# Copying z between partitions in two transfers of eight partitions instead of one of sixteen

## Chip, cores and metric

The kernel runs on one core of one Trainium2 chip. The metric is the device time of one execution in microseconds (us), less is better; three timed runs of the kernel before took 440.68, 440.70 and 441.16 us, median 440.7. Engines are named as in the profile: PE is TensorE's matmul side and PEld its weight loads, DVE is VectorE, ACT is ScalarE, POOL is GpSimd, SP is SyncE. SP computes nothing here; it only issues transfers. "16 engines" in what follows are the core's DMA engines, which carry the transfers of every queue.

## What is computed

Two stages, cut to what matters here:

```python
# stage 1: linear attention, 8 batches x 8 heads x 576 rows x 64
q_p, k_p = phi(q), phi(k)                    # exp of a projection and of its negative
kv = einsum('bhsf,bhsd->bhfd', k_p, v);  z = k_p.sum(axis=2)
x = (q_p @ kv) / (q_p @ z)                   # -> (8, 576, 512)
# stage 2: mix 64 frequencies, then add a ReLU of a channel product
X = rfft(x, axis=1)[:, :64]                  # 64 modes
Y[m] = X[m] @ (w_r[m] + 1j * w_i[m])         # one 512x512 complex matrix per mode
u = x + irfft(Y, n=576, axis=1)
out = u + relu(u @ w_ch)
```

The 64 matrices pairs `w_r`, `w_i` are 134 MB of the 164 MB that the core reads, so they stream from memory during nearly the whole kernel.

## The kernel before

**Stage 1** (lines 503 to 573) runs over 16 units (4 groups of two heads times 4 pairs of batches), and mixes of the first two channel groups are interleaved with it.

**Stage 2** (lines 779 to 1022) works on eight blocks of eight modes, `o` = 0 to 7. The weights come in tiles `wt` of 1 MB (128 partitions, bf16, cast on the way from fp32), loaded by `wload` (line 340) on POOL's queue; `next_w` (line 359) issues the next one each time that a `mix` (line 461) has used one and its buffer is free. A `mix` is eight matmuls and needs one `wt`. When the last of a block's mixes is done (`g == 3`, `i == 1`, line 943), the block's result is finished: DVE adds the partial sums into `yst` (128 partitions x 512, bf16; a partition is one of 16 mode components times one of eight batches), PE transposes it, multiplies it with `w_ch` and ACT and DVE put the product into `zst` (lines 971 to 979), of the same shape. So `yst` is Y of this block and `zst` is Y times `w_ch`.

**The copies between partitions.** The inverse transform sums over modes, so the modes of all blocks must lie along partitions and the batches beside them. `put` (line 816) does this with a transfer on SP's queue: the 128 partitions of `zst` (1 KB each) become 16 partitions of `zall`, `16 * o` to `16 * o + 15`, with the eight batches in a row (16 x 8 x 512). Each destination partition takes the rows of eight source partitions. `put` is called for `yst` into `yall` (line 952) and for `zst` into `zall` (line 980). Blocks 0 to 6 are copied so (seven copies of y, seven of z); blocks 6 and 7 also go into `yl`, block 6 on POOL's queue and block 7 on SP's.

**The readers.** `Absorb.sum_q` and `only_w` (lines 737 and 764) multiply `zall` by the tables `CI` or `CD` of the inverse transform: with 96 partitions (blocks 0 to 5) for most output rows, with 112 (block 6 too) for the first rows. The results are added to `xw`, which holds x times `w_ch`. They are in the list `todo` (line 807), which `fill` works off in portions between the mixes. PE executes in program order, so the first matmul that reads `zall` stops PE until every copy of blocks 0 to 5 has landed. The kernel ends with the output rows, added and stored by `Last` (lines 825 to 914) after the last mix.

**Order.** Every engine keeps program order (`InOrder`, line 27); a helper records all operations, so the profile names line 37 for nearly all of them and it is read by tiles. SP's queue issues, after the first loads, the copies of y and z in turn, the four of `yl`, and then the stores of the output.

The lines that the change is about:

Of the kernel before, what the change touches and what calls it, by code (L numbers as in the profile page):

```python
# [43 lines left out]
def kernel(  # L44
# [15 lines left out]
    pool, sp = InOrder(tc, nc.gpsimd), InOrder(tc, nc.sync)  # L60
# [530 lines left out]
    zall = pw.tile([128, B_, DMODEL], BF16, name="zall", tag="wt")  # L591
# [222 lines left out]
                todo.pop(0)()  # L814

    def put(src, o, dst, copies):
        if o < 7:
            sp.dma_start(dst[16 * o:16 * o + 16], src)
        if o > 5:
            for s in copies:  # L820
                r = 32 * s + 16 * (o - 6)
                (pool if o == 6 else sp).dma_start(yl[r:r + 16], src)
# [100 lines left out]
    while mixq:  # L923
        key = mixq.pop(0)
        g, o, i = key[0], key[1] // 2, key[1] % 2
# [17 lines left out]
        if g == NG - 1 and i == 1:  # L943
# [5 lines left out]
            for h in range(2):  # L949
                dve.tensor_tensor(out=yst[:, H * h:H * h + H], in0=py[:, H * h:H * h + H],  # L950
                                  in1=yacc[:, o, H * h:H * h + H], op=ALU.add)
            put(yst, o, yall, (0, 2))
            if o < 5:
                fill(min(n, 1))
# [23 lines left out]
            act.copy(zst[:, cut[0]], pz[0])  # L978
            dve.tensor_copy(zst[:, cut[1]], pz[1])
            put(zst, o, zall, (1, 3))  # L980
            fill(max(n - 2, 0) if o < 5 else n)
        else:
# [71 lines left out]
```

## Time and profile before

| | before |
|---|---|
| three timed runs, median (lowest to highest) | 440.7 us (440.68 to 441.16) |
| span of the profiled execution | 440.0 us |
| what the timed runs have over that span | 0.7 us |
| PE busy | 326.7 us, 74% |
| DVE, ACT, POOL busy | 296.0, 279.1, 112.5 us |
| HBM read, written | 163.64 MB, 9.44 MB |
| z copies into `zall` on SP | 7, 128 KB each, issued from 326.31 to 387.02 us |
| one z copy: issue on SP, issue to landing | 547 ns, 6.4 us (median) |
| first matmul that reads `zall` | 373.86 us |
| last load of a `wt`: issue, landing | 369.69 us, 404.6 us |

The span is that of one execution that the hardware profiler recorded; it gives no other time for that execution, and the timed runs are other executions. All times inside the kernel are microseconds from the start of the span. The page lists busy time by engine, the transfers by queue, and the chain of work that ended last; the timeline lists instructions in order, with the idle time before each and what ended it. The trace also keeps a record of each packet that the DMA engines moved (its queue, start, duration and bytes, but not which engine moved it) and, for each transfer, of 16 landing events.

### The profile page before, as it was taken

What the parts mean: (1) busy time and instruction counts of PE and PEld (TensorE: products, weight loads), DVE (VectorE), ACT (ScalarE), POOL (GpSimd) and SP (SyncE); (2) the same over time, 40 slices, a digit from 0 to 9 for tenths busy, and PEclk for the clock granted to TensorE, in tenths of its full rate; (3) what the DMA queues carried; (4) which work ended last, traced back from release to release, by engine and by line L of the source; (5) the groups of instructions that cost most, each with busy time, mean ns of one, the idle gap of its engine ahead of it and who ended that gap; (6) DMA issues with size and microseconds to landing.
All of it is one profiled execution on the core that took longest, in us unless ns stands there. A gap on an engine that the chain in (4) does not pass through costs nothing.

```text
span 440.0 us, 10106 instructions
## 1 busy us (share of the span) xinstructions
PE 326.7 (74%) x4190; PEld 199.7 (45%) x4233; DVE 296.0 (67%) x583; ACT 279.1 (63%) x478; POOL 112.5 (26%) x151
## 2 busy tenths in 40 slices
PE   1676668787678687778787777174679998997993
PEld 0445546555455455455455455051435454333320
DVE  5568787567785777886886878243883334885684
ACT  2788887687896777885875876210644442764782
POOL 6232132132211222221222121121101121582072
PEclk9989988689998799896896999675999999999997
DMA  8999999999999999999999999999999999996787
GB/s 193 210 211 210 237 212 238 231 217 241 235 211 239 221 230 234 237 213 235 228 221 238 210 235 209 236 209 212 212 215 223 220 221 223 206 218 150 238 361 310
DMA packets 51710, 99.55 MB, mean 226 GB/s; under 512 B 2512, under 2 KB 13648, under 8 KB 51664
## 3 DMA queue, kind: packets, MB, share of 16 engines
q0 software_dynamic: 45232, 85.86, 99.6%
q1 hardware_dynamic: 6432, 13.04, 8.5%
q8 instruction: 33, 0.54, 0.4%
q14 instruction: 13, 0.11, 0.1%
HBM read 163.64 MB, written 9.44 MB: 393 GB/s over the span
## 4 chain that ended last, share of the span: by engine, by line
PE 32%; DMA 31%; DVE 15%; ACT 15%; issue 5%; POOL 0%; POOLq 0%; ACTq 0%; DVEq 0%
DMA wt<-in_moe_w_i_dram 14%; PE pt L37 13%; PE one L37 12%; DMA wt<-in_moe_w_r_dram 8%; DMA vn<-in_v_dram 7%; ACT AB L37 6%; PE two L37 6%; DVE m L37 4%; DVE mk L37 4%; ACT AQ L37 3%; DMA qb<-in_q_dram 2%; PE pp L37 2%; ACT XT L37 2%; ACT qT L37 2%; DVE xw L37 1%
## 5 line engine op out<-in xcount | busy, mean ns | idle before, releaser
L37 ACT ACTIVATE AB<-two 128x1024 bf16<-128x1024 f32 x64 | 62.1, 1026 | 12.5 <-DVE mk L37 10.1
L37 ACT ACTIVATE AQ<-two 128x1024 bf16<-128x1024 f32 x64 | 62.7, 1046 | 1.3 <-PE two L37 1.2
L37 ACT CAST xw<-pt 128x512 bf16<-128x512 f32 x50 | 29.3, 587 | 42.3 <-PE pt L37 42.2
L37 DVE TENSOR_TENSOR va<-vn,ee 128x1152 bf16<-128x1152 f32 x32 | 42.0, 1355 | 11.9 <-DMA vn<-in_v_dram 11.9
L37 DVE TENSOR_REDUCE m<-two 128x8 f32<-128x1024 f32 x32 | 39.1, 1223 | 14.9 <-PE two L37 14.6
L37 DVE TENSOR_REDUCE mk<-two 128x8 f32<-128x1024 f32 x32 | 38.9, 1218 | 9.8 <-PE two L37 9.8
L37 POOL DMA_DIRECT2D wt<-in_moe_w_i_dram x28 | 20.9, 748 | 88.0 <-PE pt L37 36.2
L37 POOL DMA_DIRECT2D wt<-in_moe_w_r_dram x30 | 22.5, 749 | 72.3 <-PE one L37 29.3
L37 PE MATMUL pt<-wchb,xT 128*128 128x512 bf16 x127 | 34.7, 385 | 5.7 <-DVE xT L37 4.2
L37 PEld LDWEIGHTS <-xs 128*128 128x128 bf16 x624 | 31.3, 102 | 12.5 <-issue 7.5
L37 PE MATMUL two<-w2blk,qT 128*128 128x256 bf16 x128 | 21.9, 298 | 19.7 <-ACT AB L37 8.8
L37 ACT COPY qT<-one 128x512 bf16<-128x512 bf16 (+1 forms) x32 | 19.2, 641 | 26.4 <-PE one L37 26.2
L37 PE MATMUL one<-wt,XT 128*32 128x512 bf16 x304 | 27.7, 456 | 5.7 <-DMA wt<-in_moe_w_i_dram 4.1
L37 PE MATMUL one<-va,AB 64*128 64x65 bf16 x1024 | 23.1, 200 | 10.9 <-DVE va L37 10.9
L37 PEld LDWEIGHTS <-qT 128*128 128x128 bf16 x144 | 14.4, 102 | 36.7 <-issue 33.3
L37 PE MATMUL two<-mT,minus 96*128 96x512 bf16 x64 | 27.0, 423 | 3.4 <-issue 1.3
L37 DVE COPY xT<-pt 128x512 bf16<-128x512 bf16 x36 | 17.0, 472 | 17.3 <-PE pt L37 17.3
L37 PEld LDWEIGHTS <-AQ 128*128 128x128 bf16 x512 | 24.5, 108 | 8.2 <-issue 4.7
L37 PEld LDWEIGHTS <-XT 128*32 128x32 bf16 x512 | 14.7, 149 | 29.5 <-issue 23.2
L37 PE MATMUL one<-kvz,AQ 128*128 128x65 bf16 x512 | 27.2, 208 | 1.1 <-ACT qT L37 0.8
L37 DVE TENSOR_TENSOR xs<-one,rd 128x384 bf16<-128x384 f32 x48 | 26.8, 557 | 1.6
L37 PEld LDWEIGHTS <-AB 64*128 64x128 bf16 x1024 | 20.7, 101 | 15.0 <-DVE va L37 9.3
(151 smaller groups left out, 700.5 us busy)
## 6 DMA issues: line engine op xcount, KB each, us to landing
wt<-in_moe_w_r_dram POOLq DMA_DIRECT2D x30, 1024.0 KB, 28.6
wt<-in_moe_w_i_dram POOLq DMA_DIRECT2D x28, 1024.0 KB, 29.1
out_dram<-of SPq DMA_DIRECT2D x16, 512.0 KB, 3.7
vn<-in_v_dram POOLq DMA_DIRECT2D x14, 576.0 KB, 25.0
kb<-in_k_dram POOLq DMA_DIRECT2D x16, 288.0 KB, 22.0
qb<-in_q_dram POOLq DMA_DIRECT2D x16, 288.0 KB, 20.5
xs<-in_moe_w_i_dram POOLq DMA_DIRECT2D x2, 1024.0 KB, 24.1
vn<-in_v_dram SPq DMA_DIRECT2D x2, 576.0 KB, 6.7
```

The source lines that it names most:

```text
L37: ins = f(*args, **kwargs)
```

## The change

```diff
     def put(src, o, dst, copies):
-        if o < 7:
+        if o < 7 and dst is zall:
+            for h in range(2):
+                sp.dma_start(dst[16 * o + 8 * h:16 * o + 8 * h + 8], src[64 * h:64 * h + 64])
+        elif o < 7:
             sp.dma_start(dst[16 * o:16 * o + 16], src)
```

Each of the seven copies of z is issued as two transfers on SP's queue, one behind the other: the first takes source partitions 0 to 63 into the first eight destination partitions of the block, the second takes 64 to 127 into the other eight. The bytes and their places are the same, and the copies of y are as before.

In the order of instructions on the engines this adds seven transfers to SP's list, each directly behind its first half, and changes nothing else in the order of PE, DVE, ACT and POOL. The waits change in name and in number: what read `zall` or reused `zst` waited for one transfer and now waits for two.

## The prediction, made before the changed kernel was run

> **What bounds the kernel now.** I read the page first. Its third part gives the transfers by queue (packets, MB, share of 16 engines' time):
>
> ```profile
> q0 software_dynamic: 45232, 85.86, 99.6%
> q1 hardware_dynamic: 6432, 13.04, 8.5%
> q8 instruction: 33, 0.54, 0.4%
> ```
>
> q0 is POOL's queue, the inputs and weights. It is busy in 99.6% of the span, so the kernel is a stream of loads with a tail behind it. q1 is SP's queue, which carries the copies of y and z. Next the chain of work that ended last, in order of time (start, duration, what):
>
> ```profile
> 369.41 0.28 issue
> 369.69 34.91 DMA wt<-in_moe_w_i_dram
> 404.61 0.04 issue
> 404.65 0.69 PE pt L37 x8
> ```
>
> The last weight tile is issued at 369.69 and lands at 404.6, and the last mix starts at once. From there to the end are 440.0 - 404.6 = 35.4 us, in which no weight is loaded. The tile itself takes some 5 us; 35 is the queue ahead of it. So it is not its issue that counts but how fast the 16 engines work off q0. **What slows the slowest engine by 1 us puts the end 1 us later.**
>
> The landing events of that tile show how unequal the engines are: 398.0, 398.5, 398.8, 399.5, 400.0, 400.1, 400.1, 401.8 us, and then 403.2, 403.3, 403.6, 403.8, 403.8, 404.0, 404.1, 404.6. Eight engines lead, eight lag by some 4 us. The stretches of time show the same (us, busy of PE, PEld, DVE, ACT, POOL, then PEclk, DMA share, GB/s):
>
> ```profile
> 398.00:399.00 1.00, 1.00 (x6) 0.42 (x5) 0.98 (x3) 0.77 (x3) 0.78 (x1) 1.00 1.10 240
> 401.00:402.00 1.00, 1.00 (x7) 0.40 (x5) 0.60 (x2) 0.58 (x1) 0.00 (x0) 1.00 0.62 125
> 402.00:403.00 1.00, 0.36 (x2) 0.08 (x1) 0.44 (x1) 0.52 (x1) 0.00 (x0) 1.00 0.62 129
> 405.00:406.00 1.00, 0.47 (x10) 0.11 (x2) 0.64 (x2) 0.00 (x0) 0.00 (x0) 1.00 0.09 25
> ```
>
> The share is 1.10 with all engines at work and 0.62 from 401 on: nearly half of them have nothing left. The cause is in the packet records: q8's 33 packets, 16 KB and some 0.95 us each, recur in durations with a period of eight (936, 975, 975, 961, 893, 893, 948, 945 ns), so the same eight engines carry them; after each, one landing of the running tile moves back by about 1.1 us (after the first, at 33.85, one goes from 0.8 to 1.9 us behind the earliest). Four rounds make the 4 us.
>
> **What a z copy costs an engine.** The packet records around the copy at 326.31 and the others: a copy is 128 packets of 1024 bytes and 16 of 4 bytes. With 16 landing events per copy that is 8 + 1 for each engine, the packets of one destination partition. While it runs, packets of q0 and q1 alternate on an engine: q0's 2048-byte packets follow each other every 154 ns, with a z packet between them every 208. So a z packet takes 54 ns from the weights, a copy 8 x 54 + 9 = 0.44 us from each engine.
>
> **The change part by part.**
>
> *Issue.* Seven more instructions on SP, 0.55 us each. Two transfers in a row take 1.19 us (the yl copies), so the second half starts some 0.6 us after the first. Closest behind it is the copy of y at 327.85, after z at 326.31: 326.31 + 1.19 = 327.5, no delay. SP waits for other engines all through this stretch, so this costs nothing. SP also waits for the eighth transfer before its own on each semaphore; with three transfers a block instead of two that one is over two blocks (some 18 us) old, and landed. The reuse of `zst` waits for both halves, but two blocks later: nothing. With issues 2 us apart any of these would cost a part of 0.6 us.
>
> *Which engines carry a half.* No transfer in the trace has eight destination partitions, so I bound it. All of them have 16, 64 or 128, and 16 equal shares. One end: each half is again cut into 16 shares, 4 + 1 packets an engine; over both halves only the seven extra 4-byte packets are new, 7 x 9 = 63 ns. Other end: an engine takes whole destination partitions, as in the copy before. Then a half fills eight engines with 8 + 1 packets and leaves eight out, and, if the second half takes the same eight, these pay 2 x 0.44 us a copy and the others nothing. I take the second end, as the nearest row is the z copy itself, one partition to an engine. All seven copies come before the last tile has landed, so those eight engines lose 7 x 0.44 = **3.1 us**, and the other eight gain 3.1. If the halves took different eights, nothing would change but the latency.
>
> The Trainium skill states a rule for this (DMA: Bandwidth & Descriptors, "Why a DMA increments its semaphore by 16 and not by 1"): the number of engines is the largest one up to 16 that divides the outermost dimension of both sides, and on SP's queue they are the lowest-numbered. By it both halves use the same eight, which is the 3.1 us end; no row here shows it. The same page's rules for kernel authors speak the other way: two transfers to disjoint halves of the partitions are no use since both spray over all 16 engines; by that the sum is the 63 ns.
>
> *Do these eight lag or lead?* The records don't name engines. If any of them is in the lagging half, the last tile lands later by up to 3.1 us (1.7 if only the earliest of the laggards is hit: 403.2 + 3.1 - 404.6). If they are the leading eight, their last landing is 401.8 + 3.1 = 404.9 and the laggards' 404.6 - 3.1 = 401.5: 0.3 later in all. One weak row: where I could follow an engine from its landing event to its first z packet, laggards started 134 ns after the burst's first packet (mean of 11), leaders 163 (of 12). If engines are served in order, laggards stand somewhat earlier, and a transfer that fills only eight would fill the first. I take the laggards.
>
> *Latency of a copy.* It matters at one place, block 5 (start, duration, what):
>
> ```profile
> 365.06 0.55 SPq L37 DMA_DIRECT2D yall<-yst  x1
> 367.06 0.55 SPq L37 DMA_DIRECT2D zall<-zst  x1
> ```
> ```profile
> 373.52 0.41 PE L37 MATMUL pt<-yall,CI 96*64 96x512 bf16 x2 [0.57 <-DVE xs L37]
> 373.86 0.39 PE L37 MATMUL pp<-zall,CI 96*128 96x512 bf16 x1
> 403.12 0.59 PE L37 MATMUL pp<-xs,CF 128*128 128x512 bf16 x2 [0.75 <-ACT xw L37]
> 404.65 0.66 PE L37 MATMUL pt<-wt,XT 128*32 128x512 bf16 x8 [0.94 <-DMA wt<-in_moe_w_i_dram]
> ```
>
> A copy lands 6.3 to 6.6 us after its issue; its packets take the last 1.7 (8 x 208 ns). z of block 5 is there at 373.5, the first reader starts at 373.86. On the same eight engines the second half's packets follow the first's: 1.7 us later, 375.3. So PE, in program order, gets a **new wait of 1.4 us** there, with the sums of all rows and the next mixes behind it, and ACT, DVE and POOL behind those. Until the last mix PE has 0.94 + 0.22 us of waiting for weights to give back (the latter at 399.64). 0.3 us would be left. But where the last tile comes 3.1 us later, PE has those too, and the wait costs nothing. Also without the wait, PE can't gain much by weights that come early: at most the 0.94.
>
> *Sum.* Last tile 404.6 + 3.1 = 407.7. PE would be ready: copies of block 5 issued up to 1.2 us later because their weights come late, first reader 2.8 later, less 1.2 returned, still 1.5 us ahead of the tile. Behind the tile nothing changes: 35.4 us. Span 440.0 + 3.1 = 443.1; the timed runs lie 0.7 above it, 440.7 + 3.1 = **443.8 us**.
>
> **The rivals.** About 0.2% (0.9 us) is what a measurement of this kernel can tell from no change.
>
> *Laggards hit (forecast), 65%:* 442.4 to 444.8, likeliest 443.8. For it: 16 equal engines without slack in q0, and half of them or less idle at the end.
>
> *Not slower: the leading eight carry z, 20%.* Mechanism: they have 3 to 4 us to give at the last tile, and the laggards are relieved. What is left is 0.3 us of the PE wait or of the last leader: 441.0. It decides as long as the load stays under the gap of 3 to 4 us. For it: nothing in the trace says which engines lag.
>
> *The split does not concentrate, 11%:* 16 shares, or different eights. Each engine moves the same bytes; 63 ns; the two halves land about as one copy did: 440.7, at most 441.0.
>
> *Faster, 4%:* leaders carry z, no wait at 373.86, the tile early: PE's 0.94 us are returned, 439.8.
>
> **How the numbers follow.** Slower 0.65 is the first case, same 0.31 the second and third, faster 0.04. The forecast is the likeliest case; its own range is 442.4 to 444.8. The range of 8 in 10 must take in the cases near no change, from 440.5.
>
> **What would show it.** Right: each half of z with eight landings or 64 packets on half of the engines; the last `wt` landing near 407.7, its 16 landings 6 to 9 us apart where they were 6.6; a wait before the first reader of `zall`, or before mixes from 374 on, and a longer one before the last mix; a tail of 35.4 us as before. Wrong: a z half spread over 16 engines; the landings of the last tile drawn together (leaders loaded); a last tile at 404.6 with a later end, which would put the loss on PE. Everything up to 326 us must be as before.

## The result, and the profile after

The changed kernel takes 445.63 us (median of four runs, 444.89 to 447.41) where the kernel before takes 440.93 (four runs, 440.68 to 442.33). The ratio is 1.0107, with a 95% interval of 1.0084 to 1.013: 4.7 us slower. Forecast were 443.8 us, with a range of 440.5 to 444.8; the direction holds and the size does not.

The profiled execution of the changed kernel has a span of 444.1 us, 4.1 more than that of before, and a time of its own of 445.85 us. Every run for which both are listed has 1.75 us between span and time, not the 0.7 that the prediction took from two different executions. By this the profiled execution of the kernel before would have taken some 441.7 us (an estimate), 0.8 more than its median, which is why the traces differ by less than the medians.

The page's third part for the changed kernel (packets, MB, share of 16 engines):

```profile
q0 software_dynamic: 45232, 85.86, 99.0%
q1 hardware_dynamic: 6432, 13.04, 8.8%
```

Packets and bytes are the same, and the load stream is as dense as before within 0.6 points. The chain that ended last, though, no longer runs over a weight tile. The same stretch of it (start, duration, what):

```profile
366.44 7.75 DMA zall<-zst
374.19 2.06 issue
376.25 0.58 PE pp L37
...
392.28 9.23 DMA zall<-zst
401.51 0.04 issue
...
408.98 0.62 PE pt L37 x8
```

Where the last `wt` load stood (34.91 us), there are now two z copies, of block 5 and of block 6, and between them PE, DVE and ACT. So PE's order sets the end, not the weights. SP's line for the z copy of block 5, and then PE's lines around the first readers of `zall` and the mixes (in brackets the idle time before, and what ended it):

```profile
366.44 1.27 SPq L37 DMA_DIRECT2D zall<-zst  x2
```
```profile
372.92 0.41 PE L37 MATMUL pt<-yall,CI 96*64 96x512 bf16 x2 [0.56 <-DVE xs L37]
376.25 0.58 PE L37 MATMUL pp<-zall,CI 96*128 96x512 bf16 x1 [2.92 <-issue]
...
401.55 0.38 PE L37 MATMUL pt<-zall,CI 112*128 112x512 bf16 x1 [0.79 <-DMA zall<-zst]
...
408.91 0.66 PE L37 MATMUL pt<-wt,XT 128*32 128x512 bf16 x8
```

The first reader of `zall` had no wait before; it now has 2.92 us. The line puts it down to "issue", so it does not name what ended the wait; the landing events do: PE's last matmul was over at 373.3, the first half had landed by 374.2, and the second half's eight landings come from 375.55 to 376.05, just ahead of the reader. The matmul itself takes 0.58 us where it took 0.39, and the mix behind it, at 376.76, takes 1.08 where it took 0.66. The reader of block 6's copy waits 0.79 us. The last mix starts at 408.91 without a wait for its tile, where it had waited 0.94.

Why these matmuls are slower is in the granted clock. In the trace its record changes only in steps of 3.413 us. Cut along these steps, the stretches of the changed kernel are (us, busy of PE, PEld, DVE, ACT, POOL, then PEclk, DMA share, GB/s):

```profile
371.78:375.20 3.42, 0.98 (x5) 0.29 (x3) 1.89 (x3) 0.00 (x0) 0.00 (x0) 1.00 1.23 196
375.20:378.61 3.41, 2.36 (x12) 0.55 (x12) 0.00 (x0) 0.78 (x2) 0.00 (x0) 0.50 1.13 214
378.61:382.02 3.41, 3.41 (x10) 1.19 (x9) 1.29 (x2) 2.11 (x4) 0.67 (x1) 0.50 1.13 213
382.02:385.43 3.41, 3.41 (x23) 1.07 (x21) 2.88 (x5) 2.22 (x4) 2.39 (x3) 1.00 1.12 211
```
The kernel before, one step at the same place:
```profile
373.56:376.98 3.42, 3.34 (x21) 1.28 (x21) 1.87 (x4) 1.70 (x4) 0.00 (x0) 1.00 1.13 213
```

After the step in which PE stood idle, its clock is 0.50 for two steps, 6.8 us: 10 matmuls fit into a full step in place of 21 to 23. The kernel before has no half clock between 309 and 435 us. This is a second loss behind the wait, and the prediction had no term for it.

Two of the stretches that the prediction showed for the load stream, in the changed kernel:

```profile
402.00:403.00 1.00, 1.00 (x6) 0.47 (x5) 0.60 (x1) 0.55 (x1) 0.26 (x1) 1.00 0.70 133
...
405.00:406.00 1.00, 1.00 (x11) 0.39 (x12) 0.75 (x2) 0.75 (x3) 0.00 (x0) 1.00 0.28 82
```

The DMA share is 0.28 from 405 on, where it was 0.09: the stream does end later. The last tile's 16 landings are 394.7, 396.2, 399.3, 399.5, 399.6, 399.8, 401.0, 401.2, 402.8, 403.2, 403.2, 404.2, 405.3, 405.4, 405.7 and 406.8 us, spread over 12 us where it was 6.6. The last is 2.2 us later than before. PE reaches its mix 2 us after that.

**Where the 4.1 us come from.** I follow the starts of the mixes in both traces. Before and after, the second and third of them:

```profile
374.18 0.66 PE L37 MATMUL pt<-wt,XT 128*32 128x512 bf16 x8
...
378.51 0.66 PE L37 MATMUL pt<-wt,XT 128*32 128x512 bf16 x8
```
```profile
376.76 1.08 PE L37 MATMUL pt<-wt,XT 128*32 128x512 bf16 x8
...
383.11 0.66 PE L37 MATMUL pt<-wt,XT 128*32 128x512 bf16 x8
```

The one before the wait starts 0.6 us earlier than before (368.11 against 368.72), the next 2.6 later (376.76, 374.18), the third 4.6 later (383.11, 378.51); it stays at 4.6 for three more, then 5.3 (404.92, 399.64) and 4.3 (408.91, 404.65). So: the start -0.6, the wait at block 5 +3.2, the half clock +2.0 (from mix to mix 6.35 us instead of 4.33), block 6 +0.7, the last tile's wait returned -1.0, the tail -0.2. The sum is 4.1.

### The profile page after: what moved, and what is told of

It is laid out like the page before. It is cut to its first block, busy times and chain, and to the rows that moved or that the text cites. A ratio compares the mean times of both kernels' runs of the same rounds, so it can differ in the third digit from the quotient of the medians.

```text
span 444.1 us, 10124 instructions
## 1 busy us (share of the span) xinstructions
PE 331.9 (75%) x4190; PEld 201.0 (45%) x4233; DVE 296.7 (67%) x583; ACT 279.5 (63%) x478; POOL 112.8 (25%) x151
## 4 chain that ended last, share of the span: by engine, by line
DMA 40%; PE 29%; DVE 13%; ACT 9%; issue 6%; POOL 1%; POOLq 0%; SPq 0%; ACTq 0%; DVEq 0%
DMA wt<-in_moe_w_r_dram 15%; PE pt L37 14%; DMA vn<-in_v_dram 11%; PE one L37 8%; DMA kb<-in_k_dram 7%; ACT AB L37 4%; DMA zall<-zst 4%; PE two L37 4%; DMA xs<-in_moe_w_i_dram 3%; PE pp L37 3%; DVE mk L37 3%; DVE m L37 1%; DVE xw L37 1%; DVE yacc L37 1%; DVE xs L37 1%
## 5 line engine op out<-in xcount | busy, mean ns | idle before, releaser
L37 PE MATMUL two<-mT,minus 96*128 96x512 bf16 x64 | 28.3, 442 | 3.5 <-issue 1.5
L37 PEld LDWEIGHTS <-AQ 128*128 128x128 bf16 x512 | 25.5, 111 | 8.7 <-issue 5.4
L37 PE MATMUL one<-kvz,AQ 128*128 128x65 bf16 x512 | 28.1, 211 | 0.9 <-ACT qT L37 0.7
L37 DVE RECIPROCAL rd<-one 128x6 f32<-128x6 f32 x48 | 9.4, 196 | 28.1 <-PE one L37 27.9
L37 PE MATMUL one<-va,AB 64*128 64x65 bf16 x1024 | 22.2, 197 | 7.5 <-DVE va L37 7.5
```

What stands on the lines that cost most here:

```text
L37: ins = f(*args, **kwargs)
```

## The experiments

Three theories went into them. **A:** the loss is PE's, a wait at the first reader of block 5's copy and the half clock after it. **B:** the loss is the weights', held back on the eight engines that carry both halves, as predicted. **C:** every split copy costs something of its own wherever it stands, so that one costs about a seventh. The kernel before took 441.17 to 441.22 us (median) beside these runs. Unless another diff is shown, an edit is one to the condition of the changed kernel.

### Only block 5 split

```diff
-        if o < 7 and dst is zall:
+        if o == 5 and dst is zall:
```

> Only the z copy of block 5 is split. Theory A (PE's wait at the first reader of zall, 2.9 us in the changed kernel, and the half clock that follows it, set the end): the second half lands some 2 us after the first, PE waits 2 to 3 us before the first reader, matmuls take 0.6 us instead of 0.38 for some 5 us after it, and the end is 2.5 to 4.5 us later than before (443 to 445). Theory B (the weights' lateness on the eight engines sets the end, as predicted): one copy in seven, 0.44 us at most, 441.2 or less. Theory C (each additional transfer costs by itself): a seventh of the 4.7 us, 441.6.

Measured: 445.42 us, ratio 1.0098 (1.0075 to 1.012). One copy of seven gives 4.25 us of the 4.7. PE's line at the first reader, and the clock step after it:

```profile
376.10 0.38 PE L37 MATMUL pp<-zall,CI 96*128 96x512 bf16 x1 [2.51 <-DMA zall<-zst]
```
```profile
376.40:379.81 3.41, 3.41 (x16) 0.91 (x16) 0.22 (x1) 1.74 (x3) 0.00 (x0) 0.50 1.13 216
```

The trace names the z copy as what ended 2.51 us of waiting. The half clock lasts 6.8 us again. The last tile lands at 403.6 us, 1.0 earlier than before, and the last mix starts at 408.37 without a wait. B (441.2 at most) and C (441.6) fall as explanations of the main loss.

### Only blocks 0 to 4 split, twice

```diff
-        if o < 7 and dst is zall:
+        if o < 5 and dst is zall:
```

> Only the z copies of blocks 0 to 4 are split, blocks 5 and 6 whole. Theory A: no wait before the first reader of zall, no half clock; the last weight tile lands later by five sevenths of 2.2 to 3.1 us, so 1.6 to 2.2, PE has 0.9 us of that anyway and is not late itself, so the end moves by what the tile moves, 1.6 to 2.2 us (442.3 to 442.9), with a longer wait before the last mix. Theory B: five sevenths of the whole loss, 3.4 us, 444.1. Theory C: the same 3.4 us, but without a later tile.

Measured: 443.0 us (twelve runs, 441.1 to 445.0), ratio 1.0035 (1.0016 to 1.0053). There is no wait at the first reader of `zall`. PE's line at the last mix, and two clock steps around it:

```profile
404.98 0.67 PE L37 MATMUL pt<-wt,XT 128*32 128x512 bf16 x8 [0.72 <-DMA wt<-in_moe_w_i_dram]
```
```profile
403.33:406.74 3.41, 1.78 (x15) 0.78 (x15) 0.76 (x2) 0.53 (x2) 0.00 (x0) 1.00 0.13 38
406.74:410.16 3.42, 3.42 (x14) 1.56 (x12) 0.58 (x2) 1.19 (x3) 0.00 (x0) 0.50 0.33 77
```

The last mix is only 0.3 us later than before, with 0.63 and 0.51 us of waits for earlier tiles. The step with the waits around the last mix leaves PE 1.78 of 3.41 us busy, and the next step runs at half clock, in the tail, where the kernel before has none. From the last mix to the end of the span are 36.3 us instead of 35.3.

The same kernel, once more:

> Blocks 0 to 4 split once more, for another profile, since the first one (span 441.3) lies below most of its timed runs. If the loss of 1.6 us there is a later last tile: landing at 405.5 to 407 and a wait of 1 to 2.5 us before the last mix. If it is half clock that now and then follows the wait for that tile: a tile at 405 and 3 to 7 us of half clock behind it.

Measured: 441.87 us (eight runs, 441.5 to 443.5), ratio 1.0017 (1.0002 to 1.0033). The last mix starts at 404.74 after 0.74 us of waiting, and one step of half clock follows in the tail (from 406.04, after a step with PE 1.39 of 3.41 us busy). A tile at 405.5 to 407 is shown by neither profile. The medians of the two runs lie 1.1 us apart, and both profiled executions took 443.1 us, in the second run one of the two longest of eight. That the half clock in the tail comes in some executions and not in others would explain it, since a wait falls differently into the 3.4 us steps each time; this is argued from the two profiles and not shown for the timed runs.

### PE kept busy in the wait, with all seven copies split

Fourteen matmuls of 128x512 whose result nobody reads, some 3.0 us, ahead of the first reader of `zall`:

```diff
+    def warm():
+        p = banks()[:, 0]
+        for _ in range(14):
+            pe.matmul(p, lhsT=ident_b, rhs=xw[:, 2, 0, :], start=True, stop=True)
-    todo += [c.only_x for c in ab[K:]] + [c.only_w for c in ab[K:]] + [c.all for c in full]
+    todo += [c.only_x for c in ab[K:]] + [lambda: (warm(), ab[K].only_w())]
+    todo += [c.only_w for c in ab[K + 1:]] + [c.all for c in full]
```

> The changed kernel with 14 more matmuls of 128x512 (3.0 us, result read by nobody) on PE ahead of the first reader of zall. Theory A: PE is busy while it would wait, so the wait of 2.9 us shrinks to nothing or 1 us, the matmuls behind it keep 0.38 us, and the 2 us that the half clock cost come back: 443 to 444. If the half clock were no part of the loss, or not caused by the idle stretch: 445.6 as the changed kernel, or more if the added work is late itself. Theory B: 445.6.

Measured: 444.8 us, ratio 1.0088 (1.0069 to 1.0107). The first reader starts at 377.90 without a wait, the granted clock stays at 1.00, and from the mix behind the reader to the next are 4.33 us, as in the kernel before (6.35 in the changed one). That is the half clock taken away while the lateness stays. The time is 1.4 us under that of the changed kernel beside it (next run), but their intervals overlap; in this profile there are 3.4 us of half clock at 316 us, at the end of the first stage, and what follows comes 1.3 to 1.6 us later than in the changed kernel's profile (ahead of that step it was 0.2), which blurs the sum. The cleaner pair stands further down.

### The changed kernel again

> The changed kernel once more, for its spread on the same chip as the others: 445 to 446, a second half of z of block 5 that lands 2 us after the first, a wait of 2 to 3 us before the first reader of zall, and half clock behind it. Theory A expects that its time goes up and down with the length of that wait and with whether the half clock follows; theory B with the last weight tile.

Measured: 446.25 us (445.2 to 451.3), ratio 1.0134 (1.0096 to 1.0173). The wait is 2.92 us again and the half clock 6.8 us. The reader of block 6's copy has no wait in this profile (span 443.5 us), so the 0.79 us there come in one execution and not in the other.

### Only block 6 split

```diff
-        if o < 7 and dst is zall:
+        if o == 6 and dst is zall:
```

> Only the z copy of block 6 is split, which is read by the sums with 112 partitions some 8.9 us after its issue. Theory A: the second half lands 8 to 9 us after the issue, so PE waits 0 to 0.8 us there, too short for a half clock; the end is 0 to 0.8 us later (440.9 to 441.9). Theory B: 0.4 us at most. Theory C: 0.7 us.

Measured: 440.86 us, ratio 0.9992 (0.9982 to 1.0002). The reader of block 6 waits 0.23 us, nothing is lost. Half clock does not follow. In the first profile of the changed kernel the 0.79 us of block 6 are a loss because PE is what ends last; here PE has no wait for the last two tiles, for which it waited 0.22 and 0.94 us in the kernel before, and so gets the 0.23 us back.

### Quarters of four partitions, blocks 0 to 2

```diff
-        if o < 7 and dst is zall:
-            for h in range(2):
-                sp.dma_start(dst[16 * o + 8 * h:16 * o + 8 * h + 8], src[64 * h:64 * h + 64])
+        if o < 3 and dst is zall:
+            for h in range(4):
+                sp.dma_start(dst[16 * o + 4 * h:16 * o + 4 * h + 4], src[32 * h:32 * h + 32])
```

> The z copies of blocks 0 to 2 go in four transfers of four destination partitions each, the others whole. By the reading of the changed kernel's packets each quarter has four engines, always the same four, with 8 packets each: over three copies these four lose 3 x 3 x 0.44 = 3.9 us and the other twelve gain 1.3. If the four are among the leading engines, which have 3 to 4 us to give, the last weight tile lands 0 to 1.3 us earlier, and PE can use 0.9 of it: 440.0 to 441.2. If a lagging engine is among them, the last tile lands 2.5 to 3.9 us later and the end with it: 443.5 to 445. No wait at the first reader of zall in either case.

Measured: 443.7 us (442.2 to 444.45), ratio 1.0054 (1.0037 to 1.0071). The profiled execution is the fastest of them, 442.2 us. In it the last mix starts at 405.25 after 1.03 us of waiting, and the last landing of its tile comes at 405.2, the one before at 403.7. That is a tile 0.6 us later than before. Each quarter has four landings (and one early event within 1.2 us of its issue), and those of block 0, issued 0.65 to 0.85 us apart, are complete at 332.9, 334.8, 336.5 and 338.2 us: one quarter behind the other, as the same four engines would give it. Each of these then carries 3 x 4 x 0.44 = 5.3 us of z, 3.9 more than before, and a lagging one among them would have landed up to 3.9 us later. So they would be leaders; but the slower executions have no profile, and the run is inconclusive on it.

### Halves by columns

Both halves go to all 16 destination partitions, in packets of 512 bytes:

```diff
-                sp.dma_start(dst[16 * o + 8 * h:16 * o + 8 * h + 8], src[64 * h:64 * h + 64])
+                sp.dma_start(dst[16 * o:16 * o + 16, :, 256 * h:256 * h + 256],
+                             src[:, 256 * h:256 * h + 256])
```

> Each of the seven z copies in two transfers of all sixteen destination partitions, columns 0 to 255 and 256 to 511, so 512-byte packets, 16 per engine and copy instead of 8. If packets of q0 and q1 alternate one by one, whatever their size, a copy lasts 16 x (154 + 27 to 54) ns = 2.9 to 3.3 us instead of 1.7, and lands 1.2 to 1.7 us later: a wait of 0.8 to 1.4 us before the first reader of zall although all 16 engines carry it, and a tile that lands 0 to 3 us later: 441.5 to 444. If what hurts were only that eight engines carry a half, it would be 441 (no later landing).

Measured: 443.89 us, ratio 1.0061 (1.0039 to 1.0083). PE's line at the first reader, and two clock steps:

```profile
374.45 0.38 PE L37 MATMUL pp<-zall,CI 96*128 96x512 bf16 x1 [0.98 <-issue]
```
```profile
372.09:375.50 3.41, 1.78 (x13) 0.61 (x12) 1.89 (x3) 0.59 (x1) 0.00 (x0) 1.00 1.13 213
375.50:378.92 3.42, 3.42 (x9) 1.01 (x9) 1.27 (x2) 1.70 (x3) 0.00 (x0) 0.50 1.12 213
```

Each half has 16 landings, so no engine carries more bytes than in the kernel before, and yet there is a wait of 0.98 us and half clock behind it. The second half is late here too, landing 8.1 us after the first issue, but less than on eight engines (a wait of 0.98 against 2.5 to 2.9 us). It is issued 0.64 us behind the first; that the rest comes from twice the packets between those of q0 fits the expectation and is not shown.

### Block 5's second half from ACT's queue

```diff
-        if o < 7 and dst is zall:
+        if o == 5 and dst is zall:
...
-                sp.dma_start(dst[16 * o + 8 * h:16 * o + 8 * h + 8], src[64 * h:64 * h + 64])
+                (act if h else sp).dma_start(dst[16 * o + 8 * h:16 * o + 8 * h + 8],
+                                             src[64 * h:64 * h + 64])
```

> As the run with only block 5 split, but its second half is issued by ACT on its own queue, so that its packets don't stand behind those of the first half in one queue of the same eight engines. If three queues alternate on an engine, both halves end after 8 x (154 + 54 + 54) = 2.1 us instead of 1.7 for the whole copy: z lands some 0.5 to 1 us later than whole, PE waits 0 to 1 us, no half clock, end 0 to 1.5 us later than before (441 to 442.5). If the second half is late for another reason (the later issue, the load of the eight engines), it lands 2 us later as with SP alone: 445.

Measured: 442.82 us, ratio 1.0045 (1.0027 to 1.0063). The issue on ACT, the first reader on PE, and two clock steps:

```profile
366.30 1.48 ACTq L37 DMA_DIRECT2D zall<-zst  x1
```
```profile
374.15 0.38 PE L37 MATMUL pp<-zall,CI 96*128 96x512 bf16 x1 [1.00 <-DMA zall<-zst]
```
```profile
371.72:375.13 3.41, 1.83 (x14) 0.60 (x12) 1.89 (x3) 0.56 (x1) 0.00 (x0) 1.00 1.16 212
375.13:378.55 3.42, 3.35 (x9) 1.03 (x10) 1.19 (x2) 1.65 (x4) 0.00 (x0) 0.50 1.12 212
```

The wait falls from 2.51 us to 1.00: 1.5 us of the second half's lateness came from standing behind the first half on SP. This takes in its later issue: on SP the second half is issued 0.77 us after the first, on ACT at the same time, though the issue itself takes 1.48 us there. The run does not separate this from the place in the queue. The expectation denied half clock behind so short a wait; it came, and for 6.8 us. The wait of 1.00 and the 0.56 before it (for DVE, which the kernel before has too) fall into one step, which leaves PE 1.83 of 3.41 us busy.

### The filler matmuls in the kernel before, and with only block 5 split

The edit is that of the fourteen matmuls above, once made to the kernel before and once to the kernel with `o == 5`.

> The kernel before (no copy split) with the 14 matmuls of 128x512 (3.0 us, read by nobody) ahead of the first reader of zall. It gives the price of PE being 3 us late at this place without a wait and without a half clock. Theory A: PE gets 1.2 us back from its waits for weights (0.94 and 0.22), so the end is 1.8 to 2.1 us later, 442.8 to 443.3, no half clock between 374 and 400. If lateness of PE there cost all of its length: 444.2; if the kernel were bound by weights: 441.5.

> Only the z copy of block 5 split, with the 14 matmuls ahead of its reader. The wait of 2.5 us is filled by 3.0 us of work. Theory A with a half clock caused by the idle stretch: no half clock behind it, so the same time as the kernel before with those matmuls, 442.8 to 443.5, which is 2 us less than with the copy split alone (445.4). If the half clock has no share: 445 to 446.

Measured: 442.59 us, ratio 1.0032 (1.002 to 1.0044), and 442.61 us, ratio 1.0034 (1.0018 to 1.0049). PE's lines of the second one, with only block 5 split:

```profile
372.19 3.20 PE L37 MATMUL pp<-xw,ident_b 128*128 128x512 bf16 x14
375.23 0.38 PE L37 MATMUL pp<-zall,CI 96*128 96x512 bf16 x1
375.54 0.66 PE L37 MATMUL pt<-wt,XT 128*32 128x512 bf16 x8
...
379.87 0.66 PE L37 MATMUL pt<-wt,XT 128*32 128x512 bf16 x8
```
```profile
376.00:379.00 3.00, 2.84 (x16) 1.09 (x13) 1.43 (x3) 2.01 (x5) 0.04 (x1) 1.00 1.10 207
```

There is no wait behind the filler, and the clock stays at 1.00 in both. The two agree in time, and also in the trace: from the mix ahead of the filler to the last mix are 37.64 and 37.65 us. **Three us of lateness on PE cost 1.4 us in time**, the rest is taken up by what PE had to wait for later. With the filler the split of block 5 costs nothing more. Without it (445.42 us) it costs 2.8 us more, though the wait of 2.51 us is shorter than the 3.0 us of filler. In the traces, from the mix behind the reader to the next are 7.11 us without the filler and 4.33 with it: 2.8 us of half clock. Since the filler holds PE some 0.5 us longer than the wait did, the traces differ by 2.3 us from the mix ahead to the last mix (39.99 and 37.65). So of block 5's 4.25 us, about a third is the lateness and two thirds the clock.

### All but block 5 split

```diff
-        if o < 7 and dst is zall:
+        if o < 7 and o != 5 and dst is zall:
```

> All z copies split but that of block 5. Theory A: no wait before the first reader of zall; what is left is a later weight tile (2 us on the loaded laggards, less PE's 0.9) and 0 to 0.8 us at block 6: 442 to 443.5, as with blocks 0 to 4 alone (443.0). Theory B or C: 445.

Measured: 442.88 us, ratio 1.0045 (1.0026 to 1.0064). The waits are 0.32 us at the first reader, 0.54 at block 6, and 0.59 before the last mix, and there is no half clock from 374 to 434 us. The clock step with the last of these waits:

```profile
403.61:407.02 3.41, 1.89 (x16) 0.77 (x15) 0.78 (x3) 0.66 (x2) 0.00 (x0) 1.00 0.15 44
```

PE is busy for 1.89 us of this step (55%), and full clock follows; in the twin from the kernel with blocks 0 to 4 split it was 1.78 us (52%), and half clock followed. So the other six copies cost 1.7 us by the median (the profiled execution, with a span of 440.4 us, shows less of it than the median does, so what the 1.7 us consist of stays open). With block 5's 4.25 the parts add up to more than the whole, as waits do that stand in for each other.

## Why the prediction was wrong, point by point

*What bounds the kernel: right for the kernel before, not for the changed one.* The last weight tile set the end; in the changed kernel PE does. So the direction came out right mostly by luck, through a loss at block 5 (4.25 us with that copy alone) that the prediction had put at nothing.

*Issue: right.* Two issues in a row take 1.27 us on SP, and nothing on SP's list was late for it.

*Which engines carry a half: right.* Each half shows 64 packets of 1024 bytes and 8 of 4 bytes, where a whole copy has 128 and 16, and eight landings (after one early event, 1.1 us from the issue) where a whole copy has 16: eight engines with 8 + 1 packets. The second half's packets follow the first's, at block 5 the 4-byte ones ending from 374.39 to 375.52 us after those from 372.24 to 373.34. That is 2.2 us between halves that were issued 0.66 us apart, as the same eight would give it; the records do not name them. The Trainium skill's rule (DMA: Bandwidth & Descriptors, "Why a DMA increments its semaphore by 16 and not by 1") agrees with this. The same page's table "Rules for kernel authors" says that two transfers to disjoint halves of the partitions both spread over all 16 engines; the halves of eight partitions here, with eight landings each, did not.

*Do these eight lag or lead: mis-sized, and it did not matter.* The tile came 2.2 us later, not 3.1, and PE came 2 us after it. Only two engines lead far (394.7 and 396.2), eight no longer; that fits a mix of leading and lagging engines under the load, but it is argued, since the records name no engine.

*Latency of a copy: the step that failed.* It had three parts. First, "1.7 us later": the second half landed 9.3 us after the first issue (block 5 alone; 9.6 in the changed kernel) where a whole copy takes 6.3 to 6.6, so 2.8 us later. Of this some 1.5 us come from standing behind the first half on SP, later issue included, as the run from ACT's queue showed; the term missed the rest, the second half's own landing being late even from another queue, 7.7 us after its issue. Second, "new wait of 1.4 us" was 2.92 us, and 2.51 with block 5 alone. Third, "the wait costs nothing": it was priced only as time that PE stands, covered by the late tile, and not by the clock that PE has behind it. The half clock is 2.0 us in the changed kernel and 2.8 with block 5 alone. With it PE's lateness exceeds what the late tile could hide, and the whole chain changes sides. The 0.79 us of block 6 were not foreseen either; in the execution that has them, PE was on the path and had to pay them.

How would the clock have been seen? In the kernel before, PE waits 0.57 us up to 373.52, and the predicted wait of 1.4 us would begin at 373.86. A step of 3.41 us that holds both leaves PE busy for at most 1.44 us, 42%. In the profiled execution a step ends at 373.56 and would part the two, but the steps lie differently in each execution. The Trainium skill (TensorE: Matmul & The Clock Gate, "What's actually happening") says that the clock is halved after an idle window of about 3.4 us, and that the windows run free of the program. The steps of 3.413 us agree; but a step in which PE was busy for 52% or 54% was enough here, with no more than 1.0 us of idle time in one piece. The page's rule ("HAM oscillation — how this bites in real kernels") is to have no idle gaps of more than about 3.4 us; by it the 2.92 us would have been safe, and they were not.

*Not slower, faster, not concentrated: all three rivals fell.* The wait that they left at 0.3 us or nothing was there in any form of the split of block 5 that left PE idle, also with the halves by columns, where no engine had more to carry.

*Tail: right.* 35.2 us from the last mix, 35.3 before.

What is open: which engines the eight are, how often the half clock in the tail comes with blocks 0 to 4 split, and why it lasts one step there and two behind block 5. Open is also a step of half clock around 315 to 320 us that three profiles have (the filler with all copies split, the quarters, all but block 5) and that goes with 1.2 to 1.7 us of lateness behind it, against the changed kernel's profile. How often it comes in the timed runs is not known, so differences of 1 to 2 us between medians are not explained by single profiles.

No version tried is faster than the kernel before; the one with only block 6 split is equal.

## What to carry to other kernels

Before a transfer is cut in two, look at how far its landing lies ahead of its first reader (here 0.25 us: 373.61 and 373.86 in the kernel before) and take the landing of the *last* part. Here it landed 9.3 us after the first issue, where a whole copy took 6.5: with eight leading partitions instead of 16 each part had eight engines, and the second part came behind the first. Price an idle stretch on PE twice, as the wait and as the slower clock that may follow it; filling the stretch with matmuls that nobody reads is the experiment that tells the two apart. Where two engines are close to setting the end, a delay of one is free only as long as it stays under the margin, and here the second loss was what went over it.

## What the runs showed of the hardware

- The granted clock changes on a grid of 3.413 us. In the profiles of these runs between 320 and 430 us, half clock followed every step in which PE was busy for 54% or less (0.41, 0.71, 0.98, 1.39, 1.78, 1.78 and 1.83 of 3.41 us), and no step with 55% or more (1.89 and 2.09 were the lowest). Between 312 and 319 us some steps of 47% to 54% were followed by full clock, so the listed busy time is not all that counts.
- Half clock lasted two steps behind block 5 in each of five profiles (6.8 us), though PE was busy for 69% to 100% of the first of them, and one step in the tail in two.
- A transfer's issue took 1.48 us on ACT's queue (one case) and 0.55 to 0.71 us on SP's.
- A z copy, or a part of one, had as many landings as it had destination partitions, 16, 8 or 4, and the parts of one block landed one behind the other (the quarters of block 0 1.7 to 1.9 us apart).
